# Turns of rows and results placed between the groups' products, in smaller pieces, with four row buffers stored by ACT

## The chip, the cores and the metric

The kernel runs on one core of a Trainium2 chip. The metric is device time in microseconds, the median of several executions. Five engines work side by side, each in its own fixed order: PE (matrix products, with weight loads as PEld), DVE, ACT, POOL and SP, which only issues transfers. ACT issues transfers too. The transfers of both run on the core's 16 DMA engines.

## The reference

Four layers are added one after another to x, 2048 rows of 512 columns, each on the normalised x: A, B, A, B. A is a spectral filter over both axes, B a long convolution along the rows, whose kernel K comes from the parameters of a state-space model.

```python
def _A_ref(x, w_r, w_i):
    B, S, D = x.shape
    X = (lambda x, axes=(-2,-1): jnp.fft.rfft2(x, axes=axes))(x, axes=(-2, -1))
    W = w_r + 1j * w_i
    X = X * W
    y = (lambda x, s, axes=(-2,-1): jnp.fft.irfft2(x, s=s, axes=axes))(X, (S, D), axes=(-2, -1))
    return y

def _B_ref(u, A_re, A_im, B_re, B_im, C_re, C_im, log_dt, Dskip):
    ...
    P = jnp.exp(logdA[:, :, None] * l[None, None, :])
    K = jnp.einsum("dn,dnl,dn->dl", Cc, P, dB).real
    ...
    Yf = Uf * Kf[None, :, :, :]
    y = (lambda x, s, axes=(-2,-1): jnp.fft.irfft2(x, s=s, axes=axes))(Yf, (1, L2), axes=(-2, -1))[:, :, 0, :L]
    y = (lambda x, *d: x.transpose(*d))(y, 0, 2, 1) + u * Dskip[None, None, :]
    return y

x = x + _A_ref(_layernorm(x, axis=-1), A_w_r, A_w_i)
x = x + _B_ref(_layernorm(x, axis=-1), B_A_re, B_A_im, B_B_re, B_B_im, B_C_re, B_C_im, B_log_dt, B_Dskip)
x = x + _A_ref(_layernorm(x, axis=-1), A_w_r, A_w_i)
x = x + _B_ref(_layernorm(x, axis=-1), B_A_re, B_A_im, B_B_re, B_B_im, B_C_re, B_C_im, B_log_dt, B_Dskip)
```

## The kernel before

x stays in SBUF (`self.x`, 128 partitions x 16 x 512). The program has two parts: in the first (to about 346 us) the first A layer runs beside the making of K, and in the second come B, A and B. All work is written as generators ("pieces"), one per small task. A planner (`Clock.run`) holds the pieces with a rank each, estimates from a table of costs (`COST`, `LAND`, `RATE`) when each next step could start, and lets the earliest one, by rank among those that are ready, write its instructions. So the order of every engine's instructions is set when the program is built. A piece's `yield` names engines and buffers that it needs; `after(key)` waits in the plan for an event's estimated time, `emitted(key, n)` holds a step back until n such marks have been written. Neither is a wait on the chip: there the engines wait only for data and for buffers. `w(name)` takes a buffer of a ring (the `RING` tables give columns and count), `psum("a")` one of four PSUM buffers of 1024 columns.

A layer B (r = 0 for the first, called layer 1 here, r = 1 for layer 2) has two halves of 256 columns (e = 0 and 1) and in each of them eight groups (q), sixteen in all, called G0 to G15.

- `forward_b` turns a block of four row sets on PE (L771), ACT copies it to a buffer (L803), and a store sends it to DRAM (`yd`, L806, on SP). `place_b` loads it back in the groups' layout (L814, SP). This serves 128 of the columns of the first half.
- `turn_x` turns 32 other columns: PE (L787) and then a transposition by DVE (L789). There are four in the first half and eight in the second.
- `group_b`: X, the group's spectrum, on PE (L836), from the rows and a table `gi` (L866); two products with khat on DVE (L906); two sums on POOL (L912); v, the group's results, on PE (L922, two PSUM buffers); two copies on ACT (L927) and a store `vd` (L931). khat is loaded on SP (L895), four buffers or five. In layer 1's second half K's spectrum is made first: loads of yk and of a table (L884, L885), PE (L836 again), an ACT copy (L891) and a store.
- The results come back in two ways: `back_b` loads vd (L942), PE (L947), and DVE adds to x (L952); `inv_b` transposes 64 columns on DVE (L972, 2048 elements per partition), PE (L978) and DVE adds (L985). `OUT` says which columns go which way: in layer 1 all of the first half and half of the second go through `inv_b`, in layer 2 half of the second.
- `turn_k` loads the last quarter of K's rows (L1240, SP), adds a skip term (DVE, L1247), turns it on PE (L771) and stores it through ACT (L1256, L1258).
- `moments_b` takes the statistics of x (L1005), `spread` the root (ACT, L495), and the next A layer begins with `forward_a`: normalise (ACT, L511), sums and differences on POOL (L538, L540) and on DVE (L548, L549), PE (L556). Its tables are prefetched over SP (L593, L595, L665, L667) into the place of layer 1's first half.

## Time and profile before

| what | us |
|---|---|
| median of three runs | 777.3 |
| lowest, highest | 773.32, 778.66 |
| the profiled execution | 774.83 |
| its span | 773.0 |
| first A layer and K, with layer 1's first steps | 0 to 346 |
| layer 1's products | 382.0 to 472.9 |
| second A layer | about 500 to 655 |
| layer 2's products | 674.0 to 744.8 |

Times are counted from the start of the span. A row of the order of time reads: start, length of the run of equal instructions, engine, line, operation, output<-inputs, count, and in brackets how long the engine was idle before and what ended that. A row of the groups reads: line, engine, operation, shapes, count | busy us, mean ns of one | idle time before them and what ended it.

### The profile page before, as it was taken

How to read it: one execution, taken by the hardware profiler on the slowest of the kernel's cores; microseconds unless marked ns; L12 is line 12 of the kernel's file. 1: busy time of each engine (PE TensorE's matmuls, PEld its weight loads, DVE VectorE, ACT ScalarE, POOL GpSimd, SP SyncE). 2: the span in 40 equal slices, each digit the busy share in tenths (PEclk: the TensorE clock that was granted, in tenths of full speed). 3: DMA queues.
4: the chain of work that ended last, by engine and by line, in shares of the span. 5: the costliest groups of instructions: out<-in, count | busy, mean ns of one | idle time of the engine just before them, and what ended most of it. 6: DMA issues, size and time to landing. Idle time of an engine off the chain costs nothing. (4 is left out here: it accounts for less than half of the span.)

```text
span 773.0 us, 18527 instructions
## 1 busy us (share of the span) xinstructions
PE 587.4 (76%) x7588; PEld 343.5 (44%) x7588; DVE 559.9 (72%) x907; ACT 404.3 (52%) x654; POOL 280.0 (36%) x275
## 2 busy tenths in 40 slices
PE   4388887877979889885769763498887899657754
PEld 4277555545746444341424221277675544323221
DVE  5967479747776886798756984895767488696674
ACT  5676888877887888862234221185533155213220
POOL 5382256434362442330155232093534100036630
PEclk9699899988998999999888975799988899999997
DMA  9423312623442954449987482300665000648987
GB/s 335 139 83 127 104 48 82 188 68 102 119 120 84 295 163 135 135 155 308 303 244 235 139 294 77 135 2 18 223 224 199 1 2 2 204 139 277 303 263 206
DMA packets 109781, 121.46 MB, mean 157 GB/s; under 512 B 5916, under 2 KB 90912, under 8 KB 109568
## 3 DMA queue, kind: packets, MB, share of 16 engines
q1 hardware_dynamic: 68336, 93.00, 37.8%
q10 hardware_dynamic: 41360, 27.27, 11.3%
q8 instruction: 60, 0.98, 0.5%
q14 instruction: 25, 0.20, 0.1%
HBM read 80.53 MB, written 39.71 MB: 156 GB/s over the span
## 5 line engine op out<-in xcount | busy, mean ns | idle before, releaser
L912 POOL TENSOR_TENSOR apart<-wk 128x512 f32<-128x512 f32 x64 | 79.8, 1271 | 193.5 <-DVE wk L906 192.4
L1196 POOL TENSOR_TENSOR Y<-wk,Y 128x1024 f32<-128x1024 f32 x32 | 65.3, 2041 | 121.6 <-issue 69.7
L906 DVE TENSOR_TENSOR wk<-ps,wk 128x1024 f32<-128x1024 f32 x64 | 74.8, 1222 | 41.2 <-PE ps L836 15.1
L927 ACT COPY Y<-ps 128x512 f32<-128x512 f32 x64 | 34.4, 589 | 114.1 <-PE ps L922 102.8
L922 PE MATMUL ps<-apart,wk 32*64 32x256 f32 x1024 | 49.1, 442 | 35.7 <-POOL apart L912 31.9
L556 PE MATMUL ps<-cRa,wk 128*128 128x256 f32 x128 | 38.2, 425 | 36.7 <-POOL wk L538 35.4
L738 PE MATMUL ps<-cDaT,apart 128*32 128x256 f32 x256 | 59.8, 385 | 3.1 <-DVE x L753 2.4
L1181 DVE SCALAR_TENSOR_TENSOR wk<-wk,ps 128x1024 f32<-128x1024 f32 x32 | 38.8, 1213 | 23.8 <-ACT wk L1179 23.7
L1149 PE MATMUL ps<-wk,Y 96*128 96x512 bf16 x128 | 43.5, 424 | 12.5 <-DVE Y L1192 9.3
L789 DVE STREAM_TRANSPOSE Y<-ps 128x1024 f32<-128x1024 f32 x24 | 42.8, 1886 | 11.8 <-PE ps L787 11.8
L1165 ACT ACTIVATE Y<-ps 128x1024 f32<-128x1024 f32 x48 | 46.4, 1025 | 6.9 <-PE ps L1149 6.3
L922 PEld LDWEIGHTS ps<-apart,wk 32*64 32x64 f32 x1024 | 18.8, 144 | 69.2 <-POOL apart L912 59.3
L1192 DVE TENSOR_TENSOR Y<-ps,Y 128x1024 f32<-128x1024 f32 x32 | 39.0, 1218 | 11.3 <-ACT ps L1185 11.3
L1209 PEld LDWEIGHTS ps<-Y 128*32 128x32 f32 x2048 | 33.8, 119 | 26.2 <-issue 19.4
L1209 PE MATMUL ps<-Y 128*32 128x64 f32 x2048 | 39.1, 234 | 8.3 <-ACT wk L742 3.6
L538 POOL TENSOR_TENSOR wk<-wk 128x256 f32<-128x256 f32 x32 | 26.9, 840 | 51.1 <-ACT wk L511 27.1
L836 PE MATMUL ps<-Y,wk 64*32 64x256 f32 x1024 | 40.3, 431 | 5.1 <-DMA Y<-yd 1.8
L556 PEld LDWEIGHTS ps<-cRa,wk 128*128 128x128 f32 x128 | 24.5, 213 | 41.1 <-POOL wk L538 38.0
L1184 ACT ACTIVATE wk<-wk,quarter 128x1024 f32<-128x1024 f32 x32 | 36.7, 1146 | 10.2 <-DVE wk L1182 7.7
L738 PEld LDWEIGHTS ps<-cDaT,apart 128*32 128x32 f32 x256 | 26.9, 111 | 32.6 <-issue 6.2
L972 DVE STREAM_TRANSPOSE Ya<-Y 128x2048 f32<-128x2048 f32 x8 | 33.6, 4246 | 8.0 <-ACT Y L927 8.0
L1179 ACT ACTIVATE wk<-ps,magic 128x1024 f32<-128x1024 f32 x32 | 35.2, 1119 | 8.1 <-PE ps L1149 3.9
(203 smaller groups left out, 1504.3 us busy)
## 6 DMA issues: line engine op xcount, KB each, us to landing
wk<-khat SPq DMA_DIRECT2D x24, 512.0 KB, 9.3
yk<-wk ACTq DMA_DIRECT2D x32, 256.0 KB, 2.9
Ya<-vd SPq DMA_DIRECT2D x16, 512.0 KB, 7.5
Y<-in_W_dram SPq DMA_DIRECT2D x12, 515.0 KB, 4.8
x<-in_cPa_dram SPq DMA_DIRECT2D x16, 384.0 KB, 2.9
Y<-in_cGa_dram SPq DMA_DIRECT2D x12, 384.0 KB, 6.4
x<-in_W_dram SPq DMA_DIRECT2D x16, 258.0 KB, 3.6
x<-in_A_x_dram SPq DMA_DIRECT2D x8, 512.0 KB, 8.6
```

The costliest lines, as they stand in the source:

```text
L556: nc.tensor.matmul(p[:, 0:256], pq[:, 128 * i:128 * i + 128], R2[:, 128 * i:128 * i + 256], start=i == 0, stop=i == 1)
L738: nc.tensor.matmul(p[32 * i:32 * i + 32, o:o + 256], self.folded(r, i)[:, b, s2].rearrange("p g m -> p (g m)"), self.DaT[:, b, :], start=b ...
L789: self.nc.vector.transpose(self.place[e][:, :, 32 * i:32 * i + 32].rearrange("p k d -> p d k"), p.rearrange("p (w s d) -> p d s w", w=2, s ...
L836: self.nc.tensor.matmul(X[j][o:o + 32, 256 * c:256 * c + 256], G[i, j, 2 * h + c, :], y[j][i, h, :], start=True, stop=True)
L906: nc.vector.tensor_tensor(t[c], x, kh[:, :, ::-1, :] if c else kh, op=OP.mult)
L912: nc.gpsimd.tensor_tensor(Z[:, :, c], t[0][:, :, c], t[1][:, :, c], op=op)
L922: nc.tensor.matmul(v[j][64 * a:64 * a + 64, h], gi[o:o + 32, j, 4 + 2 * c:6 + 2 * c, :].rearrange("p a m -> p (a m)"), Z[o:o + 32, j, c, : ...
L1149: self.nc.tensor.matmul(p, f[:, c:c + 128], self.oh[:k, o:o + 512], start=True, stop=True)
L1165: nc.scalar.activation(m[:, :, 1024:] if i == 2 else m[:, i, :1024], p.rearrange("p (i m) -> p i m", i=2) if i == 2 else p, AF.Exp)
L1192: nc.vector.tensor_tensor(E[:, 1, :1024], p, m[:, :1024], op=OP.mult)
L1196: nc.gpsimd.tensor_tensor(E[:, 0, :1024], c, m[:, :1024], op=OP.mult)
L1209: nc.tensor.matmul(pk[32 * j:32 * j + 32, 64 * e:64 * e + 64], E1[:, r, i, :], E2[:, r, i], start=r == 0, stop=r == 1)
```

## The change

Seven things change. Turns of the second half's rows (`turn_x` with e = 1) are held back until `i` of the first half's products are written (`PACE`). Turns of results (`inv_b`) are made in pieces of 32 columns instead of 64, with four buffers of half the size, and those of the first half are held until `8 + i` products are written (`LATE`). `forward_b` in layer 1 uses four buffers instead of two, two of them taken from t2's ring, and ACT issues its store. The planner counts 0.4 us for an issue, 370 instead of 320 GB/s, a fifth less for short runs, and eight semaphores that transfers use in turn (`LANES`). `forward_a` is planned by ACT's time where DVE's stood. `HOLD` is 0 and changes nothing. The ranks of `inv_b` are new.

```diff
-RINGB = {"wo": (2048, 2), "io": (1024, 4)}
+RINGB = {"wo": (1024, 4), "io": (1024, 4)}
-COST = {"PE": (0.01, 1.69, 0.2), "DVE": (0.07, 1.05, 0.13), "ACT": (0.05, 0.84, 0.15), "POOL": (0.14, 2.12, 0.09), "SP": (0.05, 0, 0)}
-LAND, RATE = 2.0, (320e3, 210e3)
+COST = {"PE": (0.01, 1.69, 0.2), "DVE": (0.07, 1.05, 0.13), "ACT": (0.05, 0.84, 0.15), "POOL": (0.14, 2.12, 0.09), "SP": (0.4, 0, 0)}
+LAND, RATE = 2.0, (370e3, 210e3)
+SMALL = 0.8
+PACE = 1, 1
+LATE = 1, 1
+HOLD = 0
+LANES = 8
...
+                run = min(self.run_of(a) for a, _ in aps)
+                if len(self.lands) >= LANES:
+                    start = max(start, self.lands[-LANES])
+                self.land = max(self.land, start) + out.nbytes() / (RATE[both] * (SMALL if run < 1024 else 1))
                 done = self.land + LAND
+                self.lands.append(done)
...
-        yield ("DVE a" if r else "ACT a"), self.after((id(st), s2 // 4)), self.emitted(("grouped", 0, 1), 8 * r)
+        yield "ACT a", self.after((id(st), s2 // 4)), self.emitted(("grouped", 0, 1), 8 * r)
...
     def turn_x(self, r, e, i):
-        yield "PE p:a", *(self.after(("normed", r, b), 4) for b in range(4)), self.emitted(("turned", r), 4)
+        yield "PE p:a", *(self.after(("normed", r, b), 4) for b in range(4)), self.emitted(("turned", r), 4), self.emitted(("mult", r), PACE[r] * i * e)
...
     def forward_b(self, r, b):
-        ring = "iy" if r else "t1"
+        ring = "iy" if r else f"t{1 + b // 2}"
...
+        if not r:
+            self.nc.scalar.dma_start(self.pieces(self.yd[r], b, 4), y)
+            self.mark("sent", r)
+            return
...
     def inv_b(self, r, e, i):
-        yield "DVE wo", self.after(("grouped", r, e), 8), self.emitted(("rows", r, 1), 8)
-        y = self.w("wo", [128, 32, 64])
+        first = OUT[r][e] // 32
+        yield "DVE wo", self.after(("grouped", r, e), 8), self.emitted(("rows", r, 1), 8), self.emitted(("mult", r), 8 + LATE[r] * (i - first) if not e else 0)
+        y = self.w("wo", [128, 32, 32])
...
+        q = Q[:, :512]
+        for w in range(2):
+            nc.tensor.matmul(q[64 * w:64 * w + 64], self.RbT[:, w, :], y.rearrange("p (s w) d -> p s w d", w=2)[:, :, w, :], start=True, stop=True)
...
-        d = slice(256 * e + 64 * i, 256 * e + 64 * i + 64)
+        d = slice(256 * e + 32 * i, 256 * e + 32 * i + 32)
...
-                    if OUT[r][e] // 64 <= i < 4:
-                        yield o + 15 + 16 * e + 2 * i, self.inv_b(r, e, i)
+                    else:
+                        yield o + 13 + 16 * e + i, self.inv_b(r, e, i)
```

The lines after the change stand some 20 to 26 further down: L787 becomes L808, L806 L827, L814 L839, L836 L861, L866 L891, L895 L920, L906 L931, L922 L948, L972 L999, L978 L1004, L985 L1010, L1240 L1265.

SP's queue at the start of layer 1, before: cGb are the tables gi, kd the last quarter of K's rows, yd the turned rows.

```order
L866 DMA wk<-in_cGb_dram 128x512 x8
L895 DMA wk<-khat 128x4x256
L806 DMA yd_106<-wk 128x1024 x2
L1240 DMA wk<-kd_97 128x4x128
L895 DMA wk<-khat 128x4x256
L1240 DMA wk<-kd_97 128x4x128
L895 DMA wk<-khat 128x4x256 x2
L806 DMA yd_106<-wk 128x1024
L1244 DMA wk<-in_B_Dskip_dram 1x128
L806 DMA yd_106<-wk 128x1024
L1240 DMA wk<-kd_97 128x4x128
L814 DMA Y<-yd_106 128x4x128 x4
```

The same place after the change:

```order
L891 DMA wk<-in_cGb_dram 128x512
L920 DMA wk<-khat 128x4x256 x2
L1265 DMA wk<-kd_97 128x4x128 x2
L920 DMA wk<-khat 128x4x256 x2
L891 DMA wk<-in_cGb_dram 128x512
L1269 DMA wk<-in_B_Dskip_dram 1x128
L1265 DMA wk<-kd_97 128x4x128
L839 DMA Y<-yd_106 128x4x128 x4
L891 DMA wk<-in_cGb_dram 128x512
L1265 DMA wk<-kd_97 128x4x128
L839 DMA Y<-yd_106 128x4x128 x4
L920 DMA wk<-khat 128x4x256
```

The four stores are gone from SP (they stand on ACT, each behind its two copies), and six of the eight tables gi stand behind the loads that place the rows, the last five of them one by one behind a khat load.

DVE in layer 1 from the first turns of rows to the first results, before (L906 are products, two to a group; L789 turns of rows, L972 and L985 turns of results and their adds):

```order
L789 STREAM_TRANSPOSE Y<-ps 128x32x32 x8
L1247 TENSOR_TENSOR wk<-wk 1x4x32
L789 STREAM_TRANSPOSE Y<-ps 128x32x32 x3
L906 TENSOR_TENSOR wk<-ps,wk 128x1024 x2
L789 STREAM_TRANSPOSE Y<-ps 128x32x32
L906 TENSOR_TENSOR wk<-ps,wk 128x1024 x16
L972 STREAM_TRANSPOSE Ya<-Y 128x64x32 x2
L985 TENSOR_TENSOR x<-x,ps 128x16x64
L906 TENSOR_TENSOR wk<-ps,wk 128x1024 x2
L985 TENSOR_TENSOR x<-x,ps 128x16x64
L972 STREAM_TRANSPOSE Ya<-Y 128x64x32
```

After the change, from the second product on:

```order
L810 STREAM_TRANSPOSE Y<-ps 128x32x32 x2
L931 TENSOR_TENSOR wk<-ps,wk 128x1024 x4
L810 STREAM_TRANSPOSE Y<-ps 128x32x32 x2
L931 TENSOR_TENSOR wk<-ps,wk 128x1024 x4
L999 STREAM_TRANSPOSE Ya<-Y 128x32x32 x2
L931 TENSOR_TENSOR wk<-ps,wk 128x1024 x2
L1010 TENSOR_TENSOR x<-x,ps 128x16x32 x2
L999 STREAM_TRANSPOSE Ya<-Y 128x32x32
L931 TENSOR_TENSOR wk<-ps,wk 128x1024 x2
L1010 TENSOR_TENSOR x<-x,ps 128x16x32
L999 STREAM_TRANSPOSE Ya<-Y 128x32x32
L931 TENSOR_TENSOR wk<-ps,wk 128x1024 x2
```

Five turns are left ahead of the first product instead of eleven; seven stand between products, and one piece of a turn of results and one add stand between each two products of the second half, to its end. The sixteen statistics of that half stood between its products and stand behind its last one now.

DVE in layer 2, before:

```order
L789 STREAM_TRANSPOSE Y<-ps 128x32x32 x5
L906 TENSOR_TENSOR wk<-ps,wk 128x1024 x4
L789 STREAM_TRANSPOSE Y<-ps 128x32x32 x7
L906 TENSOR_TENSOR wk<-ps,wk 128x1024 x22
L952 TENSOR_TENSOR x<-x,ps 128x2x256 x4
```

And after the change:

```order
L810 STREAM_TRANSPOSE Y<-ps 128x32x32 x5
L931 TENSOR_TENSOR wk<-ps,wk 128x1024 x4
L810 STREAM_TRANSPOSE Y<-ps 128x32x32 x2
L931 TENSOR_TENSOR wk<-ps,wk 128x1024 x4
L810 STREAM_TRANSPOSE Y<-ps 128x32x32 x2
L931 TENSOR_TENSOR wk<-ps,wk 128x1024 x4
L810 STREAM_TRANSPOSE Y<-ps 128x32x32 x2
L931 TENSOR_TENSOR wk<-ps,wk 128x1024 x4
L810 STREAM_TRANSPOSE Y<-ps 128x32x32
L931 TENSOR_TENSOR wk<-ps,wk 128x1024 x8
```

The lump of seven turns behind the second group is cut into three pairs and one. On PE the order follows: v of group q, then X of group q+2, with a turn or a piece between them, now to the end of each half; before, the last groups of layer 1 had v of two groups ahead of the next X. On all engines the order of the first 346 us is changed too, in many places by a few rows, since the planner's costs are others.

More of the change, by code (lines that the diff above doesn't have):

```diff
@@ L200, in __init__ @@
         self.held, self.slots, self.land, self.piece, self.table, self.form = {}, {}, 0.0, None, "", None
-        self.pools = []
+        self.pools, self.lands = [], []
         if last:
+            self.lands = last.lands
             self.free, self.seen, self.events, self.land, self.table = last.free, last.seen, last.events, last.land, last.table
@@ L270, in meet, with run_of @@
         return False
+    @staticmethod
+    def run_of(ap):
+        dims = ap.ap if str(ap.space) == str(DRAM) else ap.ap[1:]
+        n = 1
+        for a, b in dims[::-1]:
+            if a != n and b > 1:
+                break
+            n *= b
+        return n * mybir.dt.size(ap.dtype)
     def take(self, engine, start, us):
@@ L296, in note @@
                 both = all(str(a.space) != str(DRAM) for a, _ in aps)
-                self.land = max(self.land, start) + out.nbytes() / RATE[both]
+                run = min(self.run_of(a) for a, _ in aps)
+                if len(self.lands) >= LANES:
+                    start = max(start, self.lands[-LANES])
+                self.land = max(self.land, start) + out.nbytes() / (RATE[both] * (SMALL if run < 1024 else 1))
                 done = self.land + LAND
+                self.lands.append(done)
                 self.take(engine, start, COST["SP"][0])
@@ L862, in tables @@
         for q in range(8):
-            yield "+SP gi"
+            yield "+SP gi", self.emitted(("sent", 0), HOLD * (q > 1))
             self.gi[q] = self.w("gi", [128, 2, 8, 32])
@@ L877, in group_b @@
         ring = "kh1" if r else "kh"
-        yield (f"SP {ring} yk gk" if new else "SP " + ring, turn, self.emitted(("fold", 1), 16 * r),
+        yield (f"SP {ring} yk gk" if new else "SP " + ring, turn, self.emitted(("fold", 1), 16 * r), self.emitted(("sent", 0), HOLD * (q > 1)),
                *((self.after(("turn", 1), 8),) if new else () if r else (self.after(("khat", q)),)))
@@ L907, in group_b @@
         self.drop(X, kh)
+        self.mark("mult", r)
         yield "POOL Z"
@@ L969, in inv_b @@
         nc = self.nc
-        yield "DVE wo", self.after(("grouped", r, e), 8), self.emitted(("rows", r, 1), 8)
-        y = self.w("wo", [128, 32, 64])
-        nc.vector.transpose(y.rearrange("p r d -> p d r"), self.place[e][:, :, 64 * i:64 * i + 64].rearrange("p k d -> p d k"))
+        first = OUT[r][e] // 32
+        yield "DVE wo", self.after(("grouped", r, e), 8), self.emitted(("rows", r, 1), 8), self.emitted(("mult", r), 8 + LATE[r] * (i - first) if not e else 0)
+        y = self.w("wo", [128, 32, 32])
+        nc.vector.transpose(y.rearrange("p r d -> p d r"), self.place[e][:, :, 32 * i:32 * i + 32].rearrange("p k d -> p d k"))
         yield "PE p:a"
-        q = self.psum("a")
-        y = y.rearrange("p (s w) d -> p s w d", w=2)
-        for h in range(2):
-            for w in range(2):
-                nc.tensor.matmul(q[64 * w:64 * w + 64, 512 * h:512 * h + 512], self.RbT[:, w, :], y[:, 8 * h:8 * h + 8, w, :],
-                                 start=True, stop=True)
+        Q = self.psum("a")
+        q = Q[:, :512]
+        for w in range(2):
+            nc.tensor.matmul(q[64 * w:64 * w + 64], self.RbT[:, w, :], y.rearrange("p (s w) d -> p s w d", w=2)[:, :, w, :], start=True, stop=True)
         self.drop(y)
@@ L982, in inv_b @@
         yield "DVE"
-        d = slice(256 * e + 64 * i, 256 * e + 64 * i + 64)
+        d = slice(256 * e + 32 * i, 256 * e + 32 * i + 32)
         xs = self.x[:, :, d]
         nc.vector.tensor_tensor(xs, xs, q.rearrange("p (s d) -> p s d", s=16), op=OP.add)
-        self.drop(q)
+        self.drop(Q)
         self.mark("summed", r, e)
-        self.mark("chunk", r, e, i)
-        if r and i % 2:
-            yield "SP", self.after(("chunk", r, e, i - 1))
+        self.mark("chunk", r, e, i // 4)
+        if r and i % 4 == 3:
+            yield "SP", self.after(("chunk", r, e, i // 4), 4)
             self.store_x(slice(0, 16), slice(d.stop - 128, d.stop))
@@ L994, in returns @@
     def returns(r, e):
-        return OUT[r][e] // 32 + 4 - OUT[r][e] // 64
+        return 8
     def moments_b(self, s2, e, st):
@@ L1237, in turn_k @@
         last = q == 3
-        yield "SP yk" if last else "SP KT", self.after(("stored", q))
+        yield "SP yk" if last else "SP KT", self.after(("stored", q)), self.emitted(("sent", 0), HOLD * last)
         KT = self.w("yk" if last else "KT", [128, 4, 128])
```

## The prediction

> **What bounds the kernel now.** The profiled execution took 774.83 us, 0.3% under the median of the three runs (777.3); 1.8 us of it lie outside its span of 773.0. The sum below is made against 774.83. I read the span cut into stages first (busy PE, weight load, DVE, ACT, POOL, then granted clock, DMA share, GB/s):
>
> ```profile
> 346.00:382.00 36.00, 23.11 (x138) 11.59 (x140) 28.29 (x34) 9.88 (x17) 0.00 (x0) 0.91 0.95 298
> 382.00:420.30 38.30, 29.94 (x664) 13.00 (x672) 22.91 (x20) 13.87 (x23) 19.97 (x16) 0.87 0.79 241
> 420.30:472.90 52.60, 34.41 (x608) 12.34 (x591) 42.87 (x39) 12.59 (x19) 17.45 (x14) 0.82 0.61 203
> ```
>
> No engine is full anywhere here. From 346 to 382 the DMA engines are (0.95) and POOL idles; from 420 to 473 DVE has 42.87 of 52.60 us. So the views to read next are DVE in order of time, with its waits in brackets, and after it ACT and SP for what it waits for:
>
> ```profile
> 356.92 8.75 DVE L789 STREAM_TRANSPOSE Y<-ps 128x1024 f32<-128x1024 f32 x5 [2.19 <-PE ps L787]
> 369.28 5.42 DVE L789 STREAM_TRANSPOSE Y<-ps 128x1024 f32<-128x1024 f32 x3 [3.61 <-PE ps L787]
> ...
> 381.98 2.35 DVE L906 TENSOR_TENSOR wk<-ps,wk 128x1024 f32<-128x1024 f32 x2 [1.83 <-PE ps L836]
> ...
> 417.98 2.36 DVE L906 TENSOR_TENSOR wk<-ps,wk 128x1024 f32<-128x1024 f32 x2 [2.47 <-ACT Y L927]
> 420.30 8.48 DVE L972 STREAM_TRANSPOSE Ya<-Y 128x2048 f32<-128x2048 f32 x2
> ...
> 454.13 2.35 DVE L906 TENSOR_TENSOR wk<-ps,wk 128x1024 f32<-128x1024 f32 x2 [1.44 <-PE ps L836]
> 456.41 4.33 DVE L1005 BATCH_NORM_STATS2 hm<-x 128x6 f32<-128x256 f32 x13
> 462.46 2.36 DVE L906 TENSOR_TENSOR wk<-ps,wk 128x1024 f32<-128x1024 f32 x2 [1.72 <-PE ps L836]
> 470.50 2.35 DVE L906 TENSOR_TENSOR wk<-ps,wk 128x1024 f32<-128x1024 f32 x2 [5.69 <-PE ps L836]
> 477.87 8.23 DVE L972 STREAM_TRANSPOSE Ya<-Y 128x2048 f32<-128x2048 f32 x2 [5.01 <-ACT Y L927]
> ```
>
> G0 to G15 are the sixteen groups' products (an L906 pair, 2.35 us), eight for each half of the columns: G0 starts at 381.98, G8 at 417.98, G15 at 470.50, to 472.85. Turns of rows (L789) stand in a lump ahead of G0, turns of results (L972) in the second half, and near its end DVE waits for PE (L836) three times: the groups come 8.3 and 8.0 us apart there. In layer 2 the lump of seven turns lets POOL idle 11.82 us. The next rows are DVE's, then one of POOL and two of PE:
>
> ```profile
> 665.29 8.87 DVE L789 STREAM_TRANSPOSE Y<-ps 128x1024 f32<-128x1024 f32 x5 [6.00 <-PE ps L787]
> 674.02 4.58 DVE L906 TENSOR_TENSOR wk<-ps,wk 128x1024 f32<-128x1024 f32 x4
> 678.53 12.37 DVE L789 STREAM_TRANSPOSE Y<-ps 128x1024 f32<-128x1024 f32 x7
> 690.78 4.57 DVE L906 TENSOR_TENSOR wk<-ps,wk 128x1024 f32<-128x1024 f32 x4
> ...
> 712.53 2.35 DVE L906 TENSOR_TENSOR wk<-ps,wk 128x1024 f32<-128x1024 f32 x2 [1.64 <-ACT Y L927]
> 693.26 4.95 POOL L912 TENSOR_TENSOR apart<-wk 128x512 f32<-128x512 f32 x4 [11.82 <-DVE wk L906]
> 702.28 0.69 PE L922 MATMUL ps<-apart,wk 32*64 32x256 f32 x16 [1.06 <-POOL apart L912]
> 704.12 1.09 PE L836 MATMUL ps<-Y,wk 64*32 64x256 f32 x32
> ```
>
> **The change part by part.** The new conditions in the code only set the planner's order; none is a wait on the chip of its own. (1) *Four row buffers, stored by ACT.* The third block's copy on ACT waits for the first block's store, which SP issues only after its table loads; the loads that place the rows (L814) follow at 375.93. One row of ACT, two of SP's queue, and one of PE for the price of products of 512 columns (eight in 1.94 us):
>
> ```profile
> 366.05 1.07 ACT L803 COPY wk<-ps 128x512 f32<-128x512 f32 x2 [12.51 <-DMA yd<-wk]
> 358.57 0.92 SPq L806 DMA_DIRECT2D yd<-wk  x2
> ...
> 375.93 2.29 SPq L814 DMA_DIRECT2D Y<-yd  x4
> 438.40 1.94 PE L978 MATMUL ps<-Ya,cRbT 128*64 128x512 f32 x8
> ```
>
> With four buffers nothing waits there, and the stores go out about when the first transposition starts (356.92), since PE turns these blocks ahead of it. What holds L814 next is the kd load ahead of it on SP (L1240): it waits for the first turn_k on PE, and that for the five turns now ahead of the products on DVE: 356.92 + 8.75 = 365.7, two turns on PE of 1 us (four such products), so L814 at 367.7, 8.2 us sooner, and G0 at 373.8. ACT's four issues lie in the wait that goes. What stands behind each store on ACT are the next block's copies, which PE has ready by then. Bounds: 0, if the DMA engines at 0.95 decide, and -12.5, the whole wait. I take -8.
>
> (2) *Turns between products, layer 1, first half.* G0 to G8 took 381.98 to 420.34, 38.4 us. Now DVE has 9 x 2.35 and 7 turns of 1.77 (12.37 / 7), 33.5 us, and one wait after G0: POOL 2.5 (4.95 / 2), L922 0.7, L836 1.1, less one turn, 2.5. That is 36.0, or -2.4. Against it: the tables gi3 to gi7 stand behind khat loads on SP, each of which waits for a product; X(q+3) can start when gi has landed (median below) after G(q), 5.5 to 10 us later, where G(q+3) is due 8 to 12 us later. Bounds -2.4 and +4; I take -1, since most fall short of the limit.
>
> ```profile
> wk<-khat SPq DMA_DIRECT2D x8, 512.0 KB, 9.3
> ...
> wk<-in_cGb_dram SPq DMA_DIRECT2D x8, 256.0 KB, 4.6
> ```
>
> (3) *Second half.* Each piece of a turn of results is halved. Prices from the page:
>
> ```profile
> L789 DVE STREAM_TRANSPOSE Y<-ps 128x1024 f32<-128x1024 f32 x24 | 42.8, 1886 | 11.8 <-PE ps L787 11.8
> L972 DVE STREAM_TRANSPOSE Ya<-Y 128x2048 f32<-128x2048 f32 x8 | 33.6, 4246 | 8.0 <-ACT Y L927 8.0
> L985 DVE TENSOR_TENSOR x<-x,ps 128x1024 f32<-128x1024 f32 x8 | 9.8, 1225 | 2.0 <-PE ps L978 2.0
> L952 DVE TENSOR_TENSOR x<-x,ps 128x512 f32<-128x512 f32 x16 | 10.7, 682 | 3.0 <-PE ps L947 2.9
> ```
>
> A half transposition costs 1.89 (L789, the same size) to 2.12 (half of L972); I take 2.1. A half add costs 0.68 (L952), 0.14 more in two than L985 in one. Now 8 x 2.1 + 7 x 2.35 + 7 x 0.68 = 38.0 us of DVE from G8's end to G15's end, plus 2.0 at first, since the last group of the first half needs POOL 2.5, L922 0.7 and two ACT copies (1.07, as L803's two), less G8's 2.35, before it can be turned: 40.0 against 52.5 before, -12.5. The statistics of the half (L1005, 16 in 5.4 us) move behind G15 and DVE's quoted waits for L836 (1.44 + 1.72 + 5.69 = 8.9 us) go: PE now has the spectrum of group q+2 right behind the results of group q to the end, and the last K load stands ahead of the eight table prefetches on SP instead of behind them. If all those waits stayed, it would be -3.6. PE has per group two L922 halves, two L836 and the piece's product, 1.4 + 2.2 + 1.0 = 4.6 us, under DVE's 5.1. I take -11, near the DVE end, because the two longest waits had causes that the new order takes out.
>
> (4) *End of layer 1.* ACT's last copies had 5.01 us of cover; the statistics and an add take 6.1 of it, +1.1, and turn and add now alternate, so one add waits for PE, +1.2. The prefetch of eight tables (3.4 MB by the sizes in the order, 11 us at 298 GB/s) is released by the last piece of the first half, just ahead of vd's store and loads; before, it left 27 us ahead of G15's end:
>
> ```profile
> 446.04 0.35 SPq L665 DMA_DIRECT2D Y<-in_cPa_dram  x1
> ```
>
> What is queued behind it on SP are vd's loads, and PE's L947 waits for those: 0 to +4. Together I take +3, as a piece of the tail (2.1 us each) still covers most of it.
>
> (5) *Next spectral layer.* Each normalisation follows its own root on ACT instead of the third one, so POOL can start behind the first root (493.56), and the second row's wait of DVE for POOL goes: -2 (0 to -4).
>
> ```profile
> 493.56 0.30 ACT L495 ACTIVATE rs<-mv,eps 128x4 f32<-128x4 f32 x1 [15.73 <-DVE mv L1007]
> 503.58 0.80 DVE L548 TENSOR_TENSOR wk<-wk 128x127 f32<-128x127 f32 x1 [1.82 <-POOL wk L540]
> ```
>
> (6) *Layer 2.* After G1 (678.60) come three times two turns and two products, 3.55 + 4.58 = 8.13, so G7 ends at 703.0; then one turn and G8, which waits for G6 (700.65) through POOL 2.5, L922 0.7, L836 1.1: 705.3 to 707.6. Before, G8 ended at 714.88: -7.3. From there the order repeats that of before. If each turn held one of the four PSUM buffers that a group's two results need, the pairs would wait 1.6 us three times: -2.5. I take -7.
>
> (7) *End.* DVE's work is the same, one add waits for PE, and the large store of 1 MB leaves after four pieces: +1 (0 to +2). (8) *The first 346 us* hold the same instructions, in another order on all engines, from new costs. The nearest rows of what an order cost are the waits of 3.61 and 5.69: -5 to +5; I take 0.
>
> Sum: -8 - 1 - 11 + 3 - 2 - 7 + 1 = -25, so 749.8 in the profiled manner, 0.3% more for the median: 752.
>
> **The rivals.** *The front is bound by transfers.* Share 0.95 at 298 GB/s from 346 to 382 speaks for it, 0.79 after it against. Then (1) gives nothing, (2) turns to +4 and (3) keeps half: 774.8 - 25 + 8 + 5 + 5.5 = 768.3, so 771. The Trainium skill (DMA: Bandwidth & Descriptors, section "Issuing engines are not separate DMA queues") has a rule on this side: all queues run on the same 16 DMA engines, so that another issuing engine saves only the sequencer's time. By that rule the ACT queue alone gives next to nothing, and the sum is this rival's; by the row of 12.51 us ACT waited for a store that was not yet issued, which buffers and order mend, and the sum is the forecast's. No row here shows which of the two holds once the loads come sooner.
>
> *Nothing moves, within 1%.* The first 346 us lose 5, transfers take the front and layer 2's turns cost their PSUM buffers: 774.8 - 25 + 18.5 + 5 + 4.5 = 777.8, so 780. Against it: it takes three mishaps at once.
>
> *Slower: the groups lose their overlap.* Two groups are in flight. PE works in order, and turn matmuls now stand between a group's v and the next X, with PSUM shared. If each of 21 group steps (8 and 7 in layer 1, 6 in layer 2) waits for one more transposition, 21 x 2.1 = 44: 774.8 - 25 + 44 = 793.8, so 796. From 1.2 us a step (25 / 21) it is slower. The steps of 8.3 and 8.0 us from 454.13 to 470.50 speak for it; against it, a layer 2 turn needs a buffer only until DVE reaches it, and DVE has it next.
>
> **How the numbers follow.** The forecast 0.72; transfers 0.13; nothing moves 0.08; slower 0.07. The forecast's own range: the half widths of (1) to (8), 6.2, 3.2, 4.5, 2, 2, 2.4, 1 and 5, taken as independent, add by squares to 10, so 742 to 762. To hold most of the transfers case too it reaches to 773. About 1% is what a measurement tells from no change. Faster by over 1% (under 769.5): 0.72 and half of the transfers case, 0.79; within 1%: its other half and the third case, 0.14; slower 0.07.
>
> **What would show it.** (1) G0 17 us after the first transposition instead of 25; no ACT wait for yd's store. (2), (3) products of the second half 5.1 us apart, none over 6. (4) turn of the last half 6 us after G15. (5) POOL at work before the last root. (6) POOL's pause of 11.82 gone, products in pairs 8.1 us apart. Wrong would be: waits of DVE for L836 of over 2 us per group, a stage before 346 longer by 5 us, or loads of vd later than their turn.

## The result and the profile after

The changed kernel takes 756.31 us in the median of four runs (753.39 to 759.48), the kernel before 777.32 in the four runs beside it: 0.9739 of the time, 95% interval 0.9682 to 0.9796. On another chip, in six runs (again, below), it was 0.9768 (0.9714 to 0.9822). Faster was forecast, at 752. Three executions of the experiments were disturbed, over 1.5% above the fastest of their kernel: ratios and stretches leave them out, and of out_on_sp, whose profiled execution is one of them, only the ratio is read.

The profiled execution of the changed kernel took 759.48 us, the highest of its four; its span is 757.7, against 773.0 before. So the pair of traces shows 15.3 us where the medians show 21.0.

The span of the changed kernel cut at its own marks: first turn of rows, G0, the ends of G8 and G15, the last add of layer 1, then layer 2's first turn, G8's and G15's end. The columns are those of the first fence of the prediction.

```profile
0.00:360.83 360.83, 286.03 (x3846) 178.36 (x3848) 258.24 (x449) 273.69 (x350) 143.92 (x132) 0.92 0.45 140
360.83:379.56 18.73, 10.88 (x62) 3.74 (x60) 9.10 (x7) 2.94 (x6) 0.00 (x0) 0.73 1.01 334
379.56:419.41 39.85, 31.42 (x624) 13.77 (x622) 33.68 (x25) 11.95 (x21) 19.53 (x16) 0.91 0.74 229
419.41:458.24 38.83, 30.49 (x656) 11.38 (x656) 36.34 (x30) 14.43 (x22) 18.01 (x15) 1.00 0.71 227
458.24:484.42 26.18, 14.07 (x64) 3.71 (x64) 19.18 (x30) 1.07 (x2) 2.49 (x2) 0.61 0.71 255
...
649.12:693.73 44.61, 35.48 (x614) 15.43 (x619) 42.14 (x30) 8.24 (x17) 19.85 (x16) 0.89 0.78 246
693.73:728.71 34.98, 26.04 (x464) 9.38 (x448) 21.73 (x22) 8.05 (x16) 17.45 (x14) 0.90 0.90 279
```

From G8's end to G15's end DVE is busy 36.34 of 38.83 us, where it had 42.87 of 52.60: that half is bound by DVE now. The next stretch shows what was given back: 26.18 us with DVE busy 19.18, at a granted clock of 0.61. The same cuts for the kernels that the reading below rests on, in us (the marks are read from DVE in order of time of each trace; what each kernel changes stands in the next section, and each column is one execution):

| stretch | before | changed | rows_alone | costs_alone | no_pace | big_pieces | hold_pace |
|---|---|---|---|---|---|---|---|
| start to the first turn of layer 1 | 356.9 | 360.8 | 357.2 | 367.1 | 361.0 | 356.2 | 358.5 |
| to G0 | 25.1 | 18.7 | 24.8 | 21.9 | 17.4 | 17.3 | 16.8 |
| to G8's end | 38.4 | 39.9 | 39.4 | 40.3 | 41.0 | 42.1 | 40.3 |
| to G15's end | 52.5 | 38.8 | 51.6 | 45.6 | 36.6 | 52.3 | 36.7 |
| to layer 1's last add | 18.5 | 26.2 | 18.7 | 18.7 | 25.5 | 19.2 | 21.1 |
| second A layer, to the first turn of layer 2 | 173.9 | 164.7 | 171.0 | 165.0 | 164.9 | 165.1 | 167.0 |
| to G8's end of layer 2 | 49.6 | 44.6 | 49.8 | 50.5 | 50.6 | 43.7 | 43.8 |
| to G15's end | 29.9 | 35.0 | 29.1 | 31.0 | 34.4 | 31.0 | 31.3 |
| to the end | 28.2 | 29.0 | 28.5 | 28.1 | 27.8 | 28.2 | 27.2 |

DVE of the changed kernel in order of time, at the front and in the second half:

```profile
360.83 8.82 DVE L810 STREAM_TRANSPOSE Y<-ps 128x1024 f32<-128x1024 f32 x5 [2.19 <-PE ps L808]
...
379.56 2.36 DVE L931 TENSOR_TENSOR wk<-ps,wk 128x1024 f32<-128x1024 f32 x2 [5.57 <-PE ps L861]
...
446.25 2.33 DVE L931 TENSOR_TENSOR wk<-ps,wk 128x1024 f32<-128x1024 f32 x2
451.09 2.33 DVE L931 TENSOR_TENSOR wk<-ps,wk 128x1024 f32<-128x1024 f32 x2
455.91 2.33 DVE L931 TENSOR_TENSOR wk<-ps,wk 128x1024 f32<-128x1024 f32 x2
```

The last products of the second half come 4.8 us apart without a wait (5.0 in the mean of the half); before they came 8.3 and 8.0 apart near its end. At the front DVE still waits 5.57 us for PE's spectrum. In layer 2 POOL's long pause is gone and another has come, late:

```profile
660.89 4.97 POOL L938 TENSOR_TENSOR apart<-wk 128x512 f32<-128x512 f32 x4 [68.64 <-DVE wk L931]
669.07 4.96 POOL L938 TENSOR_TENSOR apart<-wk 128x512 f32<-128x512 f32 x4 [3.21 <-PE ps L808]
...
703.90 2.48 POOL L938 TENSOR_TENSOR apart<-wk 128x512 f32<-128x512 f32 x2 [0.46 <-DVE wk L931]
716.92 4.96 POOL L938 TENSOR_TENSOR apart<-wk 128x512 f32<-128x512 f32 x4 [10.54 <-PE ps L973]
```

### The profile page after: what moved, and what is told of

It is laid out like the page before. It is cut to its first block, busy times and chain, and to the rows that moved or that the text cites. A ratio compares the mean times of both kernels' runs of the same rounds, so it can differ in the third digit from the quotient of the medians.

```text
span 757.7 us, 18552 instructions
## 1 busy us (share of the span) xinstructions
PE 584.3 (77%) x7588; PEld 334.8 (44%) x7588; DVE 554.9 (73%) x923; ACT 405.1 (53%) x654; POOL 279.4 (37%) x275
## 5 line engine op out<-in xcount | busy, mean ns | idle before, releaser
L953 ACT COPY Y<-ps 128x512 f32<-128x512 f32 x64 | 34.4, 589 | 101.5 <-PE ps L948 87.5
L931 DVE TENSOR_TENSOR wk<-ps,wk 128x1024 f32<-128x1024 f32 x64 | 74.4, 1218 | 19.1 <-PE ps L861 6.9
L948 PE MATMUL ps<-apart,wk 32*64 32x256 f32 x1024 | 47.1, 427 | 23.0 <-POOL apart L938 22.0
L1206 DVE SCALAR_TENSOR_TENSOR wk<-wk,ps 128x1024 f32<-128x1024 f32 x32 | 38.8, 1214 | 15.0 <-ACT wk L1204 14.8
L861 PE MATMUL ps<-Y,wk 64*32 64x256 f32 x1024 | 39.2, 424 | 8.6 <-ACT Y L953 4.5
L1234 PEld LDWEIGHTS ps<-Y 128*32 128x32 f32 x2048 | 34.2, 120 | 24.8 <-issue 19.1
L948 PEld LDWEIGHTS ps<-apart,wk 32*64 32x64 f32 x1024 | 19.0, 139 | 55.3 <-POOL apart L938 44.4
L1209 ACT ACTIVATE wk<-wk,quarter 128x1024 f32<-128x1024 f32 x32 | 36.7, 1147 | 11.5 <-DVE wk L1207 9.1
L999 DVE STREAM_TRANSPOSE Ya<-Y 128x1024 f32<-128x1024 f32 x16 | 33.7, 2133 | 7.4 <-ACT Y L953 7.4
```

What stands on the lines that cost most here:

```text
L861: self.nc.tensor.matmul(X[j][o:o + 32, 256 * c:256 * c + 256], G[i, j, 2 * h + c, :], y[j][i, h, :], start=True, stop=True)
L931: nc.vector.tensor_tensor(t[c], x, kh[:, :, ::-1, :] if c else kh, op=OP.mult)
L948: nc.tensor.matmul(v[j][64 * a:64 * a + 64, h], gi[o:o + 32, j, 4 + 2 * c:6 + 2 * c, :].rearrange("p a m -> p (a m)"), Z[o:o + 32, j, c, : ...
L1234: nc.tensor.matmul(pk[32 * j:32 * j + 32, 64 * e:64 * e + 64], E1[:, r, i, :], E2[:, r, i], start=r == 0, stop=r == 1)
```

## The experiments

Twelve kernels were run, four at a time on one chip, each group beside the kernel before; one of them, again, is the changed kernel a second time. Ratios are to the kernel before on the same chip, with the 95% interval.

| kernel | median, us | before, us | ratio |
|---|---|---|---|
| no_pace | 760.98 | 774.74 | 0.9816 (0.9744 to 0.9887) |
| big_pieces | 762.56 | 774.74 | 0.9828 (0.9756 to 0.9901) |
| sp_store | 757.68 | 774.74 | 0.9755 (0.9672 to 0.9838) |
| two_buffers | 757.07 | 774.74 | 0.9772 (0.9691 to 0.9852) |
| rows_alone | 776.07 | 775.85 | 1.0011 (0.9978 to 1.0044) |
| costs_alone | 764.06 | 775.85 | 0.9871 (0.9817 to 0.9925) |
| hold_tables | 755.23 | 775.85 | 0.9748 (0.9697 to 0.9798) |
| out_on_sp | 759.88 | 775.85 | 0.9769 (0.9698 to 0.9839) |
| again | 759.16 | 775.08 | 0.9768 (0.9714 to 0.9822) |
| late_back | 758.64 | 775.08 | 0.9782 (0.9734 to 0.9830) |
| hold_pace | 749.45 | 775.08 | 0.9660 (0.9609 to 0.9711) |
| all_three | 749.56 | 775.08 | 0.9661 (0.9620 to 0.9701) |

### Turns ahead of the products again

```diff
-PACE = 1, 1
+PACE = 0, 0
```

> The changed kernel with PACE = 0, 0: the turns of rows of the second half of the columns stand ahead of the products again, eight of them in layer 1 before G2 and seven in a row in layer 2; the rest is as changed. If term (6) is right, layer 2's products come in a lump again and G8 of layer 2 ends 7 us later against the end of the second spectral layer. If the turns between the products cost in layer 1 what they save there (measured: first transposition to G8's end 58.6 us after the change), that stretch stays within 2 us. Sum: 7 us slower than the changed kernel, about 763. Rival, that turns between products delay PE's next spectrum (the theory of lost overlap): layer 1's stretch gets shorter by 5 us or more and the kernel is no slower than 758.

In layer 2 the first turn to G8's end took 50.6 us, 6.0 more than in the changed kernel and 1.0 more than before: term (6) is right, and worth about 6 us. In layer 1 the turns between the products save nothing: from the first turn to G15's end it took 95.0 us, 97.4 with them. That holds over the profiles: 93.8 to 95.0 us in the three kernels with the turns ahead, 96.2 to 100.2 in the six with the turns between and small pieces. The whole, 760.98, lies between the two theories; the interval of its ratio and the changed kernel's (0.9682 to 0.9796) overlap, so the reading rests on the stretches.

### Large pieces of results again

```diff
-RINGB = {"wo": (1024, 4), "io": (1024, 4)}
+RINGB = {"wo": (2048, 2), "io": (1024, 4)}
...
-        y = self.w("wo", [128, 32, 32])
+        y = self.w("wo", [128, 32, 64])
```

The rest of `inv_b`, its ranks and its count of returns are the old ones too.

> The changed kernel with the old turns of results: pieces of 64 columns (2048 elements a lane) in two buffers, the second one of a half not held behind the products; the rest is as changed. If the small pieces make the gain of the second half (term 3, measured 13.7 us from G8's end to G15's end, of which 7.7 us are given back at the end of layer 1), G8 to G15 takes about 50 us again and the end of layer 1 falls back to about 19 us: 6 to 8 us slower than the changed kernel, about 763. Rival, that it was the K loads standing ahead of the eight table prefetches, which stay ahead here: G8 to G15 stays under 43 us and the kernel is within 2 us of the changed one.

The second half took 52.3 us again and the end of layer 1 19.2, together 6.5 us more than the 65.0 of the changed kernel; the whole is 0.9828, with an interval that overlaps the changed kernel's. But the rival wasn't ruled out as meant. The planner put the last K load behind the eight table prefetches here, so its condition did not hold. SP in order of time, its last prefetch and the K load behind it; then DVE's wait for the spectrum that needs it:

```profile
445.43 0.40 SPq L616 DMA_DIRECT2D Y<-in_W_dram  x1
447.07 0.38 SPq L909 DMA_DIRECT2D wk<-yk  x1
```

DVE of the same kernel:

```profile
463.29 4.62 DVE L931 TENSOR_TENSOR wk<-ps,wk 128x1024 f32<-128x1024 f32 x4 [6.98 <-PE ps L861]
```

The kernel with the new costs alone, further down, gives a share: there the large pieces stay, the last K load stands among the prefetches, and the half takes 45.6 us. So of the 13.7 us of this half about 6.9 came without the small pieces and about 6.8 are left to them. That the 6.9 are the place of the K load on SP is argued from these two kernels, 52.3 against 45.6; PE's order differs between them as well.

### The row buffers and their store

```diff
         self.mark("turned", r)
-        if not r:
-            self.nc.scalar.dma_start(self.pieces(self.yd[r], b, 4), y)
-            self.mark("sent", r)
-            return
         yield "SP"
         self.nc.sync.dma_start(self.pieces(self.yd[r], b, 4), y)
```

That is the edit of sp_store; two_buffers also has `ring = "iy" if r else "t1"` as before, and rows_alone is the kernel before with the new `forward_b` and nothing else.

> The changed kernel with four row buffers still, but the four stores of rows are issued by SP; nothing else moves on PE, DVE or ACT but these issues. If it is the buffers that mend the wait (ACT waited 12.51 us for a buffer), and another queue saves only issue time, the time is that of the changed kernel within 2 us (about 756). If the queue decides, since on SP the stores and the loads of rows stand behind loads of tables and of kd that wait, G0 comes 3 to 6 us later after the first transposition (18.7 us in the changed kernel) and the time is 759 to 762.

> The changed kernel with the rows as before: two row buffers, stored by SP. If term (1) is right, G0 comes about 6 to 8 us later after the first transposition (18.7 us in the changed kernel, 25.1 before) and the time is about 763. Rival, that the front is bound by the transfers of tables and K: G0 stays within 2 us and the time within 2 us of the changed kernel's 756.

> The kernel before with one part of the change alone: four row buffers, stored by ACT; costs, turns and pieces as before. If term (1) is right, the wait of 12.51 us of ACT goes, the loads of rows go out 8 us sooner and G0 comes 17 us after the first transposition instead of 25: about 769 where the kernel before takes 777. Rival, drawn from the kernel with two buffers, whose G0 came 17.9 us after the first transposition though ACT waited 7.56 us there: G0 hangs on the kd loads, the skip weights and the turns ahead of it on DVE (twelve here); then G0 stays at 24 to 26 us and the time within 2 us of the kernel before.

None of the three differs from its base by anything that was measured. With two buffers G0 came 17.9 us after the first turn, though ACT still waited 7.56 us for a buffer; sp_store had 20.5 us there and the same time in all. And rows_alone, over ten runs and thirteen of the kernel before, is 1.0011: term (1) alone gained nothing. Its own trace shows why. ACT's wait for a buffer is gone, and PE waits for the kd load instead, to the same time as before (373.06, 373.00). PE of rows_alone in order of time:

```profile
373.06 2.08 PE L771 MATMUL ps<-wk,cRb 64*128 64x512 f32 x4 [5.91 <-DMA wk<-kd]
```

SP of the same kernel, with the tables, the kd load and the loads of rows:

```profile
354.87 8.29 SPq L870 DMA_DIRECT2D wk<-in_cGb_dram  x8
363.20 0.45 SPq L899 DMA_DIRECT2D wk<-khat  x1
363.98 0.57 SPq L1244 DMA_DIRECT2D wk<-kd  x1
...
375.75 3.71 SPq L818 DMA_DIRECT2D Y<-yd  x5
```

The kd load is issued at 363.98, behind eight tables of 256 KB, and PE has it at 373.06, 9.1 us later. The loads of rows leave at 375.75, where they left at 375.93 before. In the kernel before, SP issued the kd load 4.4 us sooner, at 359.58, as it had issued the first table sooner (350.40, against 354.87 here); PE came to it at 373.00 all the same, since the turns of rows ahead of it had waited 3.26 us for ACT's late copies. What SP waited for ahead of its tables in rows_alone (us in total, times, longest):

```profile
SPq L870 <- DMA khat<-wk: 3.9, 1, 3.9
SPq L870 <- DMA yd<-wk: 1.6, 2, 1.1
```

And in the kernel before:

```profile
SPq L866 <- DMA khat<-wk: 1.5, 2, 1.1
```

The tables need nothing from these stores of khat and yd. The program's transfers use eight semaphores in turn, and with the stores of rows on ACT the turn is another: the first table waits here for a store of khat, as the fourth did before. So on the chip an engine waits for more than data and buffers, other than the part on the kernel before says, and the edit had a price of its own on SP. What the buffers would be worth without it rows_alone doesn't show. two_buffers, in the order of the changed kernel, speaks against any gain: 17.9 us with two buffers, 18.7 with four.

In the changed kernel one table stands ahead of the kd load. SP and then PE in order of time:

```profile
361.55 3.23 SPq L1265 DMA_DIRECT2D wk<-kd  x2
...
369.92 2.08 PE L792 MATMUL ps<-wk,cRb 64*128 64x512 f32 x4 [5.80 <-DMA wk<-kd]
```

From issue to PE it is 8.4 us here, nearly as long as the 9.1 of rows_alone. What differs is when SP gets to it: 0.7 us after the first turn of rows, against 6.8 in rows_alone, where the eight tables alone took SP 8.3 us to issue.

In the ten profiles of the changed kernel and its variants, SP issues one table ahead of that kd load, or two, and G0 comes 16.8 to 20.5 us after the first turn. In the three of the kernel before and its variants, where eight are ahead, it comes 21.9 to 25.1 us after it. Six or seven tables are 1.5 to 1.8 MB, by an estimate 5 to 6 us at the 315 GB/s of that stretch in the kernel before. What spreads them is an accident of the program text: the line

```diff
-            yield "+SP gi"
+            yield "+SP gi", self.emitted(("sent", 0), HOLD * (q > 1))
```

is a tuple now. The planner lets a step start ahead of the end of the one before it only where the need is a plain string with a plus (`isinstance(needs, str)`), so that each table now waits, in the plan, for the one before it to land. So this line does change something though `HOLD` is 0, other than the part on the change says. Written as a plain string again, the program of the changed kernel has the eight loads in a row, and the kernel before with the tuple has them spread. No kernel with this edit alone was run. costs_alone, which has the new costs and the eight tables in a row, took 21.9 us there; so of the 6.3 us of the front at most some 3 to 4 are left to the spread tables, and some 3 came with the order of the new costs. This share is argued from single executions and not shown.

### The planner's new costs alone

```diff
+LANES = 8
...
+                if len(self.lands) >= LANES:
+                    start = max(start, self.lands[-LANES])
...
-        yield ("DVE a" if r else "ACT a"), self.after((id(st), s2 // 4)), self.emitted(("grouped", 0, 1), 8 * r)
+        yield "ACT a", self.after((id(st), s2 // 4)), self.emitted(("grouped", 0, 1), 8 * r)
```

With the other constants of the change; turns, pieces and buffers as before.

> The kernel before with the planner's new costs and the normalisation of the second spectral layer behind its own root, without the new turns, buffers and pieces. If the new order costs the first part 3.9 us, as the profiled pair reads, the first transposition is at 361 here too. Rival: the first part differs from execution to execution (356.2 in the kernel with big pieces, whose order is the same up to there as in one with 360.8); then it lies between 355 and 359. If the second spectral layer's 6.9 us come from costs and normalisation, the stretch from the last add of layer 1 to the first turn of layer 2 is about 165 us (173.9 before, 164.7 changed), and the kernel takes about 769; if they come from what precedes it, 174 and 777.

0.9871, some 10 us: about half of what the change gives comes from the costs and the normalisation alone. The second A layer takes 165.0 us as expected of them, and the second half of layer 1 6.9 us less, which its expectation had not listed. On the first part neither number was met (367.1). That part of costs_alone, in the columns of the span cut into stages:

```profile
0.00:367.14 367.14, 293.36 (x3846) 183.85 (x3848) 257.95 (x449) 271.89 (x347) 143.82 (x132) 0.90 0.45 138
```

And big_pieces:

```profile
0.00:356.19 356.19, 281.14 (x3846) 176.55 (x3848) 259.36 (x448) 273.71 (x351) 143.91 (x132) 0.94 0.47 143
```

The number of products is the same (x3846) and PE's busy time differs by 12 us, with granted clocks of 0.90 and 0.94. So a single execution can't price the order there. Over all, the eleven profiles with the new costs have the first turn at 356.2 to 367.1, 361.4 in the mean, the two with the old costs at 356.9 and 357.2: that speaks for a price of some 4 us of the new order in the first part, though two executions of the old one are few.

### The time given back

```diff
-        yield "SP G", self.emitted(("inv", 0, 0), self.returns(0, 0)) if r else self.after(("norm", 0), 16)
+        yield "SP G", self.emitted(("back", 0, 1), 4) if r else self.after(("norm", 0), 16)
```

Here `back` is marked as each load of layer 1's results is issued; `group_a` has the same condition beside its own.

> The changed kernel with the prefetch of the second spectral layer's tables held behind the four loads of layer 1's results on SP; no other queue moves but for two adds and two turns on DVE and PE at that place. If the eight prefetches ahead of these loads are what gave back time at the end of layer 1 (the loads took 7.7 us from the last store, against 2 before), the stretch from G15's end to the last add falls from 26.2 to about 21 us, and the kernel to about 752. Rival: the tail is a chain of four turns, products and adds either way, and DVE fills the wait: the stretch stays within 1.5 us, and the time at 756.

The stretch fell to 21.0 us, as its theory had it. SP of the changed kernel in order of time, with the first and last of the eight prefetches and the loads of vd:

```profile
456.12 0.33 SPq L686 DMA_DIRECT2D Y<-in_cPa_dram  x1
...
460.97 0.62 SPq L616 DMA_DIRECT2D Y<-in_W_dram  x1
471.00 1.75 SPq L968 DMA_DIRECT2D Ya<-vd  x4
```

PE of the same kernel:

```profile
475.42 1.98 PE L973 MATMUL ps<-Ya,cRo 128*64 128x512 f32 x4 [2.45 <-DMA Ya<-vd]
```

The loads of vd on SP in the kernel before:

```profile
480.22 1.94 SPq L942 DMA_DIRECT2D Ya<-vd  x4
```

The last store of vd is issued at 463.25 in the changed kernel and at 477.87 before, so the loads behind it left 7.7 us later, against 2.4. With the prefetch held back they left 2.4 us behind the store (456.83, in hold_pace). SP of that kernel:

```profile
459.24 1.75 SPq L968 DMA_DIRECT2D Ya<-vd  x4
461.10 0.68 SPq L686 DMA_DIRECT2D Y<-in_cPa_dram  x1
```

The whole kernel, 0.9748, did not show the 5 us. In the profiled execution the first half took 44.2 us instead of 39.9, by a wait told of in the last section; whether the other three lost it there too isn't known.

```diff
-            (self.nc.sync if w else self.nc.scalar).dma_start(out[w][:, s, d], self.x[64 * w:64 * w + 64, s, d])
+            self.nc.sync.dma_start(out[w][:, s, d], self.x[64 * w:64 * w + 64, s, d])
```

> The changed kernel with all stores of the output issued by SP; ACT issues none, and no other row moves. If the out stores in ACT's queue hold up the copies behind them (a copy waited 8.10 us) and with them groups G11 to G15 of layer 2, POOL's G12 follows G11 by 8 us instead of 13, and G15's end follows G8's by 30 instead of 35 us: about 751. Rival: POOL waits there for PE, and PE for the load of results (3.34 us at its first such product), which no store's queue changes: G8 to G15 stays within 1.5 us, and the end, with half of its last stores behind others on SP, is 0 to 2 us later: 756 to 758.

0.9769: no gain. The time shows no price of the stores in ACT's queue.

```diff
-        yield "PE p:a"
+        yield "PE p:a", self.emitted(("v", r), 12 * r * (1 - e))
         Q = self.psum("a")
```

> The changed kernel itself, beside the three below on the same chip, as their measure: about 756, 0.974 of the kernel before. If the first part's 3.9 us of the profiled pair are the granted clock of one execution (0.92 against 0.93 over that part) and no price of the order, the first transposition comes anywhere between 356 and 364 here.

> The changed kernel, with the products of the first half's results in layer 2 held on PE until twelve groups have given their results. If what gives time back there is PE's order (the first such product waits 3.34 us for its load, with the results of G10 and G11 and the spectrum of G12 behind it), the stretch from G8's end to G15's end falls from 35.0 to about 31 us and the kernel to about 752.5. Rival: the DMA engines bind that stretch (share 0.90 in the changed kernel, 0.97 before), or the products only move and hold up G13 to G15 instead; then it stays at 33 to 35 us and the time at 756.

The changed kernel's first turn came at 363.8 here, at the edge of what was given. Holding the products is no gain either: 0.9782 against 0.9768 of the changed kernel on the same chip. The stretch took 32.6 us, and POOL's waits only moved, behind G12 and G14:

```profile
713.14 4.97 POOL L938 TENSOR_TENSOR apart<-wk 128x512 f32<-128x512 f32 x4 [5.03 <-DVE wk L931]
723.38 2.48 POOL L938 TENSOR_TENSOR apart<-wk 128x512 f32<-128x512 f32 x2 [5.27 <-DVE wk L931]
```

The rival holds, in its half that the products only move. With the changed kernel's order there the stretch takes 31.3 and 31.8 us where the granted clock is 0.95 (hold_pace, sp_store), and 34.0 to 35.0 in the five profiles where it is 0.90. PE's first products of results tell the two apart. PE of the changed kernel:

```profile
704.45 1.97 PE L973 MATMUL ps<-Ya,cRo 128*64 128x512 f32 x4 [3.34 <-DMA Ya<-vd]
```

And of hold_pace:

```profile
692.95 1.08 PE L973 MATMUL ps<-Ya,cRo 128*64 128x512 f32 x4 [1.87 <-DMA Ya<-vd]
```

In all five PE waits 3.0 to 3.3 us for the load of vd at this place, and the four products behind the wait take 1.97 or 1.98 us; in the other two it waits 1.8 and 1.9 us, and they take 1.08. So the longer wait comes first and the lower clock behind it. What makes the load late isn't shown, nor is the wait the whole of it: all_three, where these products are held as in late_back and wait for nothing, took 34.6 us at 0.95. The share of the DMA engines (0.90 to 0.96) was not changed by itself.

```diff
-PACE = 1, 1
+PACE = 0, 1
```

> The changed kernel with the table prefetch held behind the loads of layer 1's results, and the turns of layer 1 ahead of the products again (PACE = 0, 1). If the two stages read in their own kernels hold together, the end of layer 1 takes 21 us instead of 26, first transposition to G15's end 95 instead of 97.4: 7 us less than the changed kernel, about 749. Rival: what is held back is lost again, since the second spectral layer then waits for its tables or the granted clock falls by as much; then the stretch from the last add of layer 1 to the first turn of layer 2 is over 168 us (164.7) and the time within 2 us of the changed kernel.

> Both edits of the kernel above and the products of layer 2 held on PE. If the three causes are separate, their gains add up: 5 + 2.4 + 4 = 11 us less than the changed kernel, about 745. Rival, as for its parts: no more than the better one of the two other kernels, 749 to 756.

hold_pace, the table prefetch held and turns between products in layer 2 alone, takes 749.45 us, 9.7 less than the changed kernel beside it, where its theory said 7; its interval, 0.9609 to 0.9711, just clears 0.9714 to 0.9822. Its stretches in layer 1:

```profile
358.53:375.33 16.80, 12.13 (x74) 4.86 (x72) 14.43 (x10) 1.99 (x4) 0.00 (x0) 0.90 0.98 322
375.33:415.63 40.30, 27.63 (x635) 11.95 (x642) 28.28 (x22) 13.19 (x23) 19.95 (x16) 1.00 0.85 267
415.63:452.28 36.65, 29.05 (x648) 11.70 (x632) 36.37 (x30) 13.85 (x21) 17.70 (x14) 1.00 0.64 203
452.28:473.39 21.11, 11.75 (x64) 3.03 (x64) 18.96 (x30) 1.07 (x2) 2.49 (x2) 0.75 0.70 253
```

From the first turn to G15's end it is 93.8 us (97.4 in the changed kernel's first profile, 99.7 in the second), and the end of layer 1 21.1. The second A layer took 2.3 us more (167.0); why is open, since hold_tables, with the same tables held, took 165.0. The third edit adds nothing (749.56), as late_back had shown. hold_pace is the best of the kernels.

## Why the prediction was right, and where it was not

The sign and the size were right, 756.3 in a range of 742 to 773 about 752. Several terms were not, and they made up for one another. Against the profiled pair, term by term:

- **(1) Row buffers, -8.** The front did become 6.3 us shorter, and G0 came 18.7 us after the first turn, near the 17 given as a sign, but not by this: that was luck. Alone the part gave 1.0011 (0.9978 to 1.0044), and undone it changed nothing. The step that failed: PE's first turn_k, and with it the loads of rows, was said to wait for the five turns on DVE, 8.75 us from the first one, and the kd load that turn_k reads was put at nothing. In the changed kernel PE starts it 9.1 us after the first turn, but out of a wait of 5.80 us for that load; in hold_tables it starts at 371.21, ahead of the end of the five turns on DVE (371.74). In rows_alone, where SP issued the load 6.8 us after the first turn and not 0.7, it is 15.9 us. The order of SP that stands with the change shows the tables spread; the prediction priced that as a cost in (2) and not as a gain here. The Trainium skill's rule on this term (DMA: Bandwidth & Descriptors, section "Issuing engines are not separate DMA queues") was the better guide: another queue saves only the time of issuing. The runs agree, 0.9755 with SP's stores against 0.9739 with ACT's.
- **(2) Turns between products in layer 1, -1.** Measured +1.5 in the stretch, and without these turns front and both halves together took 95.0 instead of 97.4 us. A miss by 2 to 3 us.
- **(3) Second half, -11.** Measured -13.7. Both causes named were there: smaller pieces under DVE's bound (about 6.8), and the last K load ahead of the prefetches, which with the rest of the new costs' order is about 6.9 (costs_alone). DVE's bound was 5.1 us a product, measured 5.0 in the mean and 4.8 at the end.
- **(4) End of layer 1, +3.** Measured +7.7: the mechanism was named (loads of vd queued behind the eight tables), its size was not; 0 to +4 was allowed for it, and hold_tables gave 5.2 back. Of the signs given for being wrong, loads of vd later than their turn is the one that came: PE waited 2.45 us for them.
- **(5) Second A layer, -2.** In the same cuts it is -9.2. The row before its first product, which is what the term spoke of, gained 1.6; the rest lies further in, with the granted clock up. The span cut from the last add to the first product and from there to the first add, in the kernel before:

```profile
491.35:531.06 39.71, 30.08 (x157) 23.95 (x158) 30.59 (x72) 25.52 (x60) 23.42 (x34) 0.87 0.01 1
531.06:615.18 84.12, 68.27 (x556) 54.38 (x555) 56.48 (x155) 32.17 (x117) 32.54 (x45) 0.88 0.45 153
```

The changed kernel:

```profile
484.42:522.49 38.07, 28.74 (x157) 25.31 (x158) 28.11 (x73) 25.87 (x60) 23.22 (x34) 0.87 0.01 2
522.49:601.33 78.84, 62.64 (x556) 49.98 (x555) 56.14 (x155) 32.21 (x117) 32.47 (x45) 0.96 0.47 163
```

The same 556 products take PE 5.6 us less at 0.96. The layer took 173.9 and 171.0 us in the two profiled kernels with the old costs, and 164.7 to 168.8 in the eleven with the new, so the gain is there; how much of it is order and how much clock was not separated.
- **(6) Layer 2, -7.** To G8's end it is -5.0 in the pair and -6.0 against no_pace; POOL's pairs come 8.15 us apart, as forecast 8.13. But 5.1 us were lost from G8 to G15, which the prediction took for unchanged ("from there the order repeats that of before"). It does not: PE's first product of results stands one group earlier, where it waits 3.34 us for its load (0.17 before). On paper, G8's chain adds to 705.0 and not 705.3, which changes nothing here.
- **(7) End, +1.** Measured +0.8. **(8) First 346 us, 0.** Measured +3.9 in the pair and some 4 in the mean of eleven, within the -5 to +5 allowed; that the order is what costs it rests on two executions of the old one.

The sum in the profiled pair: 3.9 - 6.3 + 1.5 - 13.7 + 7.7 - 9.2 + 0.8 in the stretches named, less 5.0 and plus 5.1 in layer 2's two: -15.2, of 15.3. The medians' 21.0 against the 25 forecast is nearer than the terms deserve: without the second A layer's 7 us more than forecast, the misses of (4), (6) and (8) would have shown.

Of the rivals, transfers at the front came nearest for term (1), since a load and not a buffer holds the front, and missed in time, since it took the order of the loads as fixed. Lost overlap did not come: no product of the second half waits over 2 us, and of the first half's products behind G0 only G1 waits longer than before, 4.09 us (2.88 before). Nothing moves was wrong.

## What to carry to other kernels

Before a wait for a buffer is priced, look at what its engine needs next and which transfer that stands behind: here the buffer came free and the next load, behind 2 MB of tables and a wait for a store that it does not need, took the wait over whole. When prefetches are released by an event on the critical path, put the loads that the path needs ahead of them in the queue; that was worth 5 us in its stretch here. And a part that is undone alone and done alone tells more than a sum that fits: this sum fitted with its first term at zero.

## What was not expected of the hardware

The spread between executions goes with the granted clock. The eleven runs of the kernel before in the last group go from 769.82 us at 0.912 to 780.78 at 0.890. Within one kernel it falls behind waits. PE of the changed kernel at the end of layer 1, two groups of four equal products, the first without a wait and the second after one of 4.12 us:

```profile
456.77 1.08 PE L1004 MATMUL ps<-Ya,cRbT 128*64 128x512 f32 x4
...
466.24 1.98 PE L1004 MATMUL ps<-Ya,cRbT 128*64 128x512 f32 x4 [4.12 <-DVE Ya L999]
```

The Trainium skill (TensorE: Matmul & The Clock Gate, Part 1) says that PE's clock is gated by how busy PE has lately been, down to half. The trace agrees in direction and size, 1.98 against 1.08 us; so a wait ahead of PE can cost its own length and then slower products.

A landing 2 us later can cost twice that. In the changed kernel PE waited 1.07 us for K's first table; in hold_tables, with the same order, 3.07, and the turns behind it ran at half speed, here each with the row that follows it, PE of the changed kernel:

```profile
408.35 1.10 PE L861 MATMUL ps<-wk 64*32 64x256 f32 x32 [1.07 <-DMA wk<-in_cGk_dram]
409.38 1.99 PE L808 MATMUL ps<-Ya,cRf 64*128 64x512 f32 x8
```

And in hold_tables:

```profile
410.39 1.96 PE L861 MATMUL ps<-wk 64*32 64x256 f32 x32 [3.07 <-DMA wk<-in_cGk_dram]
412.28 3.78 PE L808 MATMUL ps<-Ya,cRf 64*128 64x512 f32 x8
```

The first half of layer 1 took 39.9 us in the one and 44.2 in the other. The slower clock does not follow each time. In again, the changed kernel a second time, PE waited longer there and the turns ran at full speed:

```profile
412.59 1.10 PE L861 MATMUL ps<-wk 64*32 64x256 f32 x32 [3.34 <-DMA wk<-in_cGk_dram]
413.62 1.99 PE L808 MATMUL ps<-Ya,cRf 64*128 64x512 f32 x8
```

Its half took 43.2 us all the same.
